# Four unused tiles that shift SBUF addresses in a fused attention and expert-layer kernel

## The chip, the cores and the metric

The kernel runs on one core of a Trainium2 chip. The metric is device time in microseconds (us) of one execution. It is given as the median of three runs. The profile is of one further execution of the same program, with its own time.

## What is computed

The reference is three layers in a row, all in fp32:

```python
# attention: B=2, H=8, S=768, D=64; key kept if pos < n_sink (4) or 0 <= rel < window (128)
scores = np.where(keep, scale * q @ k.T, -1e9)
a = softmax(scores);  x = a @ v                    # -> x: 1536 tokens x 512
# layer 1
h = (x @ w1) * (x @ w2) @ w3;  x = h @ w_out       # 512 -> 1024 -> 1024 -> 512
# layer 2
h = x @ w_in                                       # 512 -> 2048
g = np.maximum(h, 0.0) + np.log1p(np.exp(-np.abs(h)))   # softplus
return g @ w_out                                   # 2048 -> 512
```

The weights reach the chip as 64-bit floats and are decoded there.

## The kernel before

The program has an attention part and four dense stages. TensorE runs them one after the other.

- **Attention** (`attention`, to about 74 us): eight pairs of heads. Scores `s` (line 381), masking on VectorE (386), exponential on ScalarE (393), division on GpSimd (407), transposes (420) and the product with the values `xt` (456). A planner with a table of offsets sets this order.
- **Stage 1** (`stage1`): `ab` = (x w1)(x w2), 24 blocks of 24 matmuls. **Stage 2** (`stage2`): the product w34 of w3 and w_out, 8 blocks of 24. **Stage 3** (`stage3`): `x2p` = ab w34, 12 blocks of 24. **Stage 4** (`stage4`): `h` = y w_in, 48 blocks of 12, softplus on ScalarE, GpSimd and VectorE, and the output products `ox` and `o`, 48 times 12.

Every dense product is made by `mm3` (lines 164 to 168). Both operands are split into a high and a low part in the type fp32r, and three matmuls are issued per tile of 128 rows: high by high (166), high by low (167), low by high (168). There are 576 + 192 + 288 + 576 + 576 = 2,208 of these matmuls, each with 512 moving columns (2 KB a partition, read in a row) and 128 stationary columns (512 bytes a partition). So the start of either operand has the same remainder by 512 as the start of its tile; this remainder is called the rest from here on.

**Where tiles lie.** Tiles come from pools, and a pool is placed as a stack. On the left side lie `slots` (the tiles of x, later y and the output, and then those of w34) and, after the attention, `slots_ab` (ab, w_out's parts, later most of w_in and w_out of layer 2). On the right side, from the top down, lie `dec` (buffers in which weights are decoded), `ring` (five buffers `u` for decoded weights, then `bs` and `pr`) and `att` (all of the attention's tiles). After stage 3 the ring is released and `sp` (the softplus tiles spa, spu, spl, gh, gl) takes its place. All tiles of the dense stages are multiples of 2 KB, and before the change each of them starts at a rest of 480 bytes.

**Late reuse of the ring.** In stage 3 weights for stage 4 are decoded into ring buffers ahead of time (`w4_early`). When the slots come free, `w4_split` (682 to 686) copies them there: ScalarE writes the high part, VectorE the low part, both from the ring. Softplus tiles that lie on a ring buffer can't be written before that is done.

The lines of softplus are 704 (abs), 705 (exp), 706 (one plus it, on GpSimd), 709 (log), 711, 714 and 717 (VectorE), 720 (high part) and 151 (low part of anything, in VectorE).

Of the kernel before, what the change touches and what calls it, by code (L numbers as in the profile page):

```python
# [9 lines left out]
F32 = mybir.dt.float32  # L10
# [10 lines left out]
P = 128  # L21
# [38 lines left out]
    P=(-697.11, -455.77, -631.6, -474.64, -647.58, -395.71), PV=(97.88, 94.31, 94.22, 97.88, 97.88, 169.98),  # L60
# [81 lines left out]
class Net:  # L142
# [723 lines left out]
    def net(self, banded):  # L866
        tc = self.tc

        def sb(name, side="left"):
            return tc.alloc_tile_pool(name=name, bufs=1, side=side, reuse_waits="tile")  # L870

        psum = tc.alloc_tile_pool(name="psum", bufs=1, space=PSUM)
        self.slots = sb("slots")
        self.x = [[self.slot(SLOT_X + t * NC + c, f"x{t}_{c}") for c in range(NC)] for t in range(NCH)]
        self.dec = sb("dec", "right")
        self.ring = sb("ring", "right")
        att = sb("att", "right")

        if banded:
            with tc.manual_schedule():  # L880
                self.attention(att, psum)
        else:
            self.dense_attention(att, psum)
            self.last_load = ()
            self.first = self.w12_unit(0)
            self.gate = ()
        att.release()
        self.slots_ab = sb("slots_ab")
        self.w4, self.early = {}, {}
        self.stages12(self.ring, psum)  # L890
        self.stage3(psum)
        self.ring.release()
        sp = sb("sp", "right")
        self.stage4(sp, psum)
        sp.release()
        self.dec.release()
        self.slots_ab.release()
        self.slots.release()
        psum.release()
# [69 lines left out]
```

## Time and profile before

| | |
|---|---|
| median of three runs | 583.76 us (583.74 to 584.16) |
| the profiled execution | 584.81 us |
| its span, first to last instruction | 582.9 us |
| TensorE busy | 573.5 us (98%) |
| VectorE busy | 431.0 us (74%) |
| ScalarE busy | 347.1 us (60%) |
| GpSimd busy | 82.4 us (14%) |
| mean granted TensorE clock | 0.998 of the upper level |

The profile names engines PE (TensorE matmuls), PEld (TensorE weight loads), DVE (VectorE), ACT (ScalarE), POOL (GpSimd) and SP (SyncE). A duration is that of one instruction from its start to its modelled end; since matmuls are pipelined, the distance from start to start tells their rate, not the duration.

### The profile page before, as it was taken

How to read it: one execution, taken by the hardware profiler on the slowest of the kernel's cores; microseconds unless marked ns; L12 is line 12 of the kernel's file. 1: busy time of each engine (PE TensorE's matmuls, PEld its weight loads, DVE VectorE, ACT ScalarE, POOL GpSimd, SP SyncE). 2: the span in 40 equal slices, each digit the busy share in tenths (PEclk: the TensorE clock that was granted, in tenths of full speed). 3: DMA queues.
4: the chain of work that ended last, by engine and by line, in shares of the span. 5: the costliest groups of instructions: out<-in, count | busy, mean ns of one | idle time of the engine just before them, and what ended most of it. 6: DMA issues, size and time to landing. Idle time of an engine off the chain costs nothing.

```text
span 582.9 us, 9844 instructions
## 1 busy us (share of the span) xinstructions
PE 573.5 (98%) x3718; PEld 472.8 (81%) x3718; DVE 431.0 (74%) x906; ACT 347.1 (60%) x712; POOL 82.4 (14%) x162
## 2 busy tenths in 40 slices
PE   9999999999999999999999999999999999999996
PEld 6888788888888888888888777888888888888885
DVE  6889899999989976767988889845644554654553
ACT  7999967667566754545666668544444344444352
POOL 4657700000000000000000221111111011011010
PEclk9999999999999999999999999999999999999999
DMA  7566645454445523342643221000200000200002
GB/s 275 172 221 195 188 140 149 139 151 151 133 144 148 164 88 108 114 140 72 201 128 106 74 72 37 0 1 0 73 0 2 0 1 1 73 0 1 0 1 79
DMA packets 15512, 54.51 MB, mean 94 GB/s; under 512 B 1888, under 2 KB 1888, under 8 KB 15456
## 3 DMA queue, kind: packets, MB, share of 16 engines
q1 hardware_dynamic: 15168, 53.27, 29.3%
q8 instruction: 31, 0.51, 0.4%
q10 hardware_dynamic: 288, 0.52, 0.3%
q14 instruction: 25, 0.20, 0.1%
HBM read 50.64 MB, written 3.15 MB: 92 GB/s over the span
## 4 chain that ended last, share of the span: by engine, by line
PE 86%; POOL 4%; DVE 3%; ACT 3%; issue 2%; DMA 1%; SPq 0%; POOLq 0%; DVEq 0%
PE ab L166 8%; PE ab L168 7%; PE ab L167 7%; PE h L167 6%; PE h L168 6%; PE h L166 6%; PE x2p L168 4%; PE x2p L166 4%; PE x2p L167 4%; PE ox L168 3%; PE o L167 3%; PE o L168 3%; PE o L166 3%; PE ox L167 3%; PE ox L166 3%; PE w34p L168 2%
## 5 line engine op out<-in xcount | busy, mean ns | idle before, releaser
L706 POOL TENSOR_SCALAR spu<-spa 128x512 f32<-128x512 f32 (+1 forms) x49 | 35.9, 733 | 458.7 <-ACT spa L705 458.7
L151 DVE TENSOR_TENSOR gl<-spl,gh 128x512 fp32r<-128x512 f32 x47 | 32.6, 694 | 76.8 <-ACT gh L720 76.5
L704 ACT ACTIVATE spa<-h 128x512 f32<-128x512 f32 (+1 forms) x49 | 28.7, 586 | 86.5 <-PE h L168 86.3
L166 PE MATMUL ab<-x,u_w 128*128 128x512 f32 x192 | 74.8, 390 | 0.0
L167 PE MATMUL ab<-x,u_w 128*128 128x512 f32 x192 | 74.7, 389 | 0.0
L168 PE MATMUL ab<-x,u_w 128*128 128x512 f32 x192 | 74.7, 389 | 0.0
L166 PE MATMUL h<-y,w4h 128*128 128x512 f32 x192 | 74.7, 389 | 0.0
L167 PE MATMUL h<-y,w4h 128*128 128x512 f32 x192 | 74.7, 389 | 0.0
L168 PE MATMUL h<-y,w4l 128*128 128x512 f32 x192 | 74.7, 389 | 0.0
L193 ACT ACTIVATE dt_w<-raw_w 128x512 bf16<-128x512 bf16 x64 | 42.5, 669 | 52.1 <-DMA raw_w<-w4d 16.9
L201 DVE SCALAR_TENSOR_TENSOR dc_w<-raw_w,dt_w 128x512 uint16<-128x512 uint16 x64 | 44.2, 697 | 10.1 <-ACT dt_w L196 9.6
L196 ACT ACTIVATE dt_w<-dt_w,rebias 128x512 uint16<-128x512 uint16 x64 | 45.8, 721 | 1.3
L711 DVE SCALAR_TENSOR_TENSOR spu<-spu,spa 128x512 f32<-128x512 f32 (+1 forms) x49 | 33.3, 680 | 16.6 <-ACT spl L709 16.6
L709 ACT ACTIVATE spl<-spu 128x512 f32<-128x512 f32 (+1 forms) x49 | 30.4, 623 | 24.5 <-POOL spu L706 24.5
L407 POOL TENSOR_SCALAR e<-e,st 128x196 f32<-128x196 f32 (+1 forms) x96 | 39.5, 434 | 23.4 <-ACT e L393 17.1
L393 ACT ACTIVATE e<-e,st 128x196 f32<-128x196 f32 (+1 forms) x96 | 42.2, 447 | 0.9 <-DVE st L386 0.7
L168 PEld LDWEIGHTS ab<-x,u_w 128*128 128x128 f32 x192 | 36.1, 188 | 7.5
L167 PEld LDWEIGHTS h<-y,w4h 128*128 128x128 f32 x192 | 36.1, 188 | 7.5
L167 PEld LDWEIGHTS ab<-x,u_w 128*128 128x128 f32 x192 | 36.0, 188 | 7.5
L166 PEld LDWEIGHTS h<-y,w4h 128*128 128x128 f32 x192 | 36.0, 188 | 7.5
L166 PEld LDWEIGHTS ab<-x,u_w 128*128 128x128 f32 x192 | 36.0, 188 | 7.4
L168 PEld LDWEIGHTS h<-y,w4l 128*128 128x128 f32 x192 | 36.0, 188 | 7.4
(127 smaller groups left out, 1306.4 us busy)
## 6 DMA issues: line engine op xcount, KB each, us to landing
raw_w<-w4d SPq DMA_DIRECT2D x32, 511.8 KB, 4.2
raw_w<-w SPq DMA_DIRECT2D x16, 511.8 KB, 4.6
raw_w<-w3t SPq DMA_DIRECT2D x16, 511.8 KB, 3.8
qk<-qk SPq DMA_DIRECT2D x7, 792.0 KB, 4.5
raw_wo<-wod SPq DMA_DIRECT2D x8, 511.8 KB, 3.8
v<-vu SPq DMA_DIRECT2D x8, 400.0 KB, 5.5
v<-v SPq DMA_DIRECT2D x8, 384.0 KB, 4.6
out<-os SPq DMA_DIRECT2D x10, 256.0 KB, 2.3
```

The costliest lines, as they stand in the source:

```text
L151: return engine.tensor_tensor(out=lo, in0=x, in1=hi.bitcast(F32), op=ALU.subtract)
L166: nc.tensor.matmul(ps, lhs[0], rhs[0], start=start, stop=False)
L167: nc.tensor.matmul(ps, lhs[0], rhs[1], start=False, stop=False)
L168: nc.tensor.matmul(ps, lhs[1], rhs[0], start=False, stop=stop)
L193: return nc.scalar.activation(t.bitcast(BF), x["top"].bitcast(BF), AF.Abs)
L196: return nc.scalar.activation(x["t"], x["t"], AF.Relu, bias=self.rebias[:, 0:1], scale=8.0)
L201: nc.vector.scalar_tensor_tensor(out=c, in0=x["top"], scalar=0x8000, in1=t, op0=ALU.bitwise_and, op1=ALU.bitwise_or)
L393: nc.scalar.activation(e, e, AF.Exp, bias=st[:, 0, i : i + 1], scale=-1.0, accum_out=st[:, 1, i : i + 1])
L407: nc.gpsimd.tensor_scalar(out=e, in0=e, scalar1=buf("st", h)[:, 2, i : i + 1], scalar2=1.0, op0=ALU.mult, op1=ALU.mult)
L706: nc.gpsimd.tensor_scalar(out=u[:, c], in0=a[:, c], scalar1=1.0, scalar2=1.0, op0=ALU.add, op1=ALU.mult)
L709: nc.scalar.activation(l[:, c], u[:, c], AF.Ln)
L711: nc.vector.scalar_tensor_tensor(out=u[:, c], in0=u[:, c], scalar=1.0, in1=a[:, c], op0=ALU.subtract, op1=ALU.subtract)
```

## The change

Four tiles are allocated that no instruction reads or writes: 64 bytes a partition behind x in `slots`, 128 bytes at the start of `slots_ab`, 256 bytes at the end of `ring`, and 128 bytes at the end of `sp`.

```diff
         self.x = [[self.slot(SLOT_X + t * NC + c, f"x{t}_{c}") for c in range(NC)] for t in range(NCH)]
+        self.slots.tile([P, 16], F32, name="pad_w34")
         self.dec = sb("dec", "right")
...
         self.slots_ab = sb("slots_ab")
+        self.slots_ab.tile([P, 32], F32, name="pad_ab")
         self.w4, self.early = {}, {}
         self.stages12(self.ring, psum)
         self.stage3(psum)
+        self.ring.tile([P, 64], F32, name="pad_ring")
         self.ring.release()
         sp = sb("sp", "right")
         self.stage4(sp, psum)
+        sp.tile([P, 32], F32, name="pad_sp")
         sp.release()
```

The addresses of the two built programs differ like this (bytes of a partition):

| tiles | moved by | rest before | rest after |
|---|---|---|---|
| x, y, output; decode buffers | 0 | 480 | 480 |
| w34; layer 2's weights 12 to 15 | +64 | 480 | 32 |
| ab; w_out's parts; layer 2's weights 0 to 11 | +192 | 480 | 160 |
| ring buffers u, bs, pr | -256 | 480 | 224 |
| all attention tiles (qk, e, pt, v, ident, masks) | -256 | many | each by 256 other |
| softplus tiles | -128 | 480 | 352 |

Moving and stationary operand, which both had the rest 480 in every dense product, now have 480 and 224 (stage 1), 160 and 224 (stage 2), 160 and 32 (stage 3), 480 and 160 or 32 (`h`), 160 or 32 and 352 (`ox`, `o`).

On all five engines the instructions stand in the same order as before, with the same operands. One wait is new. It stands on ScalarE, at the start of stage 4, ahead of the second softplus tile (`spa0_1`; the number behind a name is only a count of tiles). Before:

```order
L157 CAST y2_3_3703<-x2p2_3_3704 128x512 [waits PE_49]
L704 ACTIVATE spa0_0_3764<-h0_0_3751 128x512 [waits DVE_49,PE_49]
L705 ACTIVATE spa0_0_3764<-spa0_0_3764 128x512 [waits Activation_49]
L709 ACTIVATE spl0_0_3766<-spu0_0_3765 128x512 [waits Pool_49]
L704 ACTIVATE spa0_1_3789<-h0_1_3776 128x512 [waits PE_49]
L705 ACTIVATE spa0_1_3789<-spa0_1_3789 128x512 [waits Activation_49]
```

And on the same engine, at the same place, now:

```order
L157 CAST y2_3_3705<-x2p2_3_3706 128x512 [waits PE_49]
L704 ACTIVATE spa0_0_3767<-h0_0_3754 128x512 [waits DVE_49,PE_49]
L705 ACTIVATE spa0_0_3767<-spa0_0_3767 128x512 [waits Activation_49]
L709 ACTIVATE spl0_0_3769<-spu0_0_3768 128x512 [waits Pool_49]
L704 ACTIVATE spa0_1_3792<-h0_1_3779 128x512 [waits DVE_49,PE_49]
L705 ACTIVATE spa0_1_3792<-spa0_1_3792 128x512 [waits Activation_49]
```

Nothing moved; line 704 on `spa0_1` now waits for VectorE too. The pools `ring` and `sp` no longer start at the same address, so this tile reaches 128 bytes into a second ring buffer, and has to wait until VectorE's `w4_split` of layer 2's weight 11 (the last of the twelve) has read it.

## Rows read from the trace of the kernel before

**Rows 1.** Span and mean granted TensorE clock of the core.

```profile
core 0: 582.9 us, clock 0.998
```

**Rows 2.** Stretches: us, busy us (instructions) of each engine, PEclk, DMA share, GB/s.

```profile
core 0: us, PE busy (x) PEld busy (x) DVE busy (x) ACT busy (x) POOL busy (x), PEclk, DMA share, GB/s
0.00:74.20 74.20, 71.22 (x1511) 58.99 (x1512) 61.89 (x292) 66.80 (x248) 46.12 (x113) 1.00 0.67 212
74.20:313.50 239.30, 239.30 (x1056) 198.22 (x1057) 207.65 (x370) 148.03 (x239) 0.31 (x1) 1.00 0.45 136
...
318.00:360.00 42.00, 40.90 (x176) 32.08 (x175) 36.57 (x61) 28.73 (x50) 10.80 (x9) 1.00 0.20 64
360.00:577.60 217.60, 217.60 (x960) 179.78 (x958) 120.73 (x181) 101.17 (x175) 24.96 (x40) 1.00 0.03 12
577.60:583.00 5.40, 0.01 (x1) 0.00 (x0) 0.69 (x1) 0.00 (x0) 0.00 (x0) 0.80 0.36 126
```

**Rows 3.** Groups of weight loads by shape: busy us, mean ns, idle before.

```profile
L166 PEld LDWEIGHTS ab<-x,u_w 128*128 128x128 f32 x192 | 36.0, 188 | 7.4
L420 PEld LDWEIGHTS pt<-ident,e 128*128 128x128 f32 x96 | 13.5, 141 | 2.1 <-POOL e L407 1.1 <-issue 0.5
L420 PEld LDWEIGHTS pt<-ident,e 128*68 128x68 f32 x80 | 9.0, 112 | 5.2 <-POOL e L407 2.8 <-issue 1.1 <-ACT pt L432 0.7
```

**Rows 4.** Single lines of the attention: duration ns, min/median/max, then first and last start.

```profile
L420 PEld LDWEIGHTS pt<-ident,e x176: 109/138/145, 10.9 to 71.1; 128*128 128x128 f32 x96, 128*68 128x68 f32 x80
L386 DVE CUSTOM_DVE_ANT_0 e<-s,bias x80: 248/356/364, 5.0 to 63.7; 128x196 f32<-128x196 f32 x64, 128x128 f32<-128x128 f32 x16
L407 POOL TENSOR_SCALAR e<-e,st x96: 370/428/939, 10.1 to 70.1; 128x196 f32<-128x196 f32 x80, 128x128 f32<-128x128 f32 x16
```

**Rows 5.** Line 151 on VectorE, several tiles: duration ns, min/median/max.

```profile
L151 DVE TENSOR_TENSOR gl<-spl,gh x47: 678/695/697, 322.5 to 569.5; 128x512 fp32r<-128x512 f32 x47
L151 DVE TENSOR_TENSOR u_w<-dr_w,u_w x30: 680/684/694, 79.0 to 216.0; 128x512 fp32r<-128x512 f32 x30
...
L151 DVE TENSOR_TENSOR y<-x2p,y x12: 681/684/693, 255.5 to 316.3; 128x512 fp32r<-128x512 f32 x12
```

**Rows 6.** VectorE in order of time, end of stage 3: start us, length us.

```profile
311.75 4.62 DVE L151 TENSOR_TENSOR w4l<-w4e,w4h 128x1024 fp32r<-128x1024 f32 x4
316.28 0.68 DVE L151 TENSOR_TENSOR y<-x2p,y 128x512 fp32r<-128x512 f32 x1
```

**Rows 7.** ScalarE in order of time, start of stage 4.

```profile
318.49 0.63 ACT L709 ACTIVATE spl<-spu 128x512 f32<-128x512 f32 x1 [0.74 <-POOL spu L706]
319.21 0.60 ACT L704 ACTIVATE spa<-h 128x512 f32<-128x512 f32 x1
```

**Rows 8.** GpSimd in order of time, start of stage 4.

```profile
323.61 0.62 POOL L706 TENSOR_SCALAR spu<-spa 128x512 f32<-128x512 f32 x1 [2.43 <-ACT spa L705]
329.53 3.12 POOL L706 TENSOR_SCALAR spu<-spa 128x512 f32<-128x512 f32 x1 [5.30 <-ACT spa L705]
...
341.96 3.05 POOL L706 TENSOR_SCALAR spu<-spa 128x512 f32<-128x512 f32 x1 [5.72 <-ACT spa L705]
...
354.31 0.64 POOL L706 TENSOR_SCALAR spu<-spa 128x512 f32<-128x512 f32 x1 [5.72 <-ACT spa L705]
```

**Rows 9.** Stretches of five us inside stage 4's start, columns as in rows 2.

```profile
345.00:350.00 5.00, 4.88 (x22) 3.69 (x20) 3.71 (x6) 3.83 (x7) 0.66 (x2) 1.00 0.31 119
350.00:355.00 5.00, 4.73 (x20) 3.62 (x21) 4.88 (x10) 4.21 (x9) 0.64 (x1) 1.00 0.00 0
355.00:360.00 5.00, 4.37 (x20) 3.29 (x19) 4.93 (x9) 3.36 (x6) 0.99 (x1) 1.00 0.34 108
```

**Rows 10.** A wait alone, on GpSimd's sequencer, line 706: ns, min/median/max.

```profile
L706 POOLq EVENT_SEMAPHORE  x47: 17/17/17, 316.4 to 565.3; - x47
```

## The prediction

> **What bounds the kernel now.** I read the granted clock first: one core, 0.998 of the upper level, so there is no disturbance to allow for [rows 1]. Then the stretches [rows 2]. From 74.2 to 313.5 us TensorE has no gap: 1,056 matmuls, which is exactly stages 1 to 3 (576 + 192 + 288), in 239.30 us. That is 226.6 ns from one start to the next. From 360 to 577.6 us there are 960 in 217.60 us, 226.7 ns each. So for 457 of 582.9 us the time is a count of matmuls times one number, and nothing that another engine does can shorten it. What is left is the attention, where TensorE stands still for 3.0 us of 74.2, the start of stage 4 (318 to 360 us, 1.1 us of standing still), and the end (5.4 us, one copy and the last store). The change counts if it changes the 226.7 ns, or lengthens something in these three places.
>
> **Part 1: the addresses of the 2,208 matmuls.** The change removes and adds no work. Its term is 2,208 times the difference in the start-to-start distance. What in the profile says whether that distance depends on rests? In the dense stages nothing can directly, because every one of the 2,208 has the same pair, 480 and 480. Three things bear on it from the side.
>
> First, other engines. In the long stretch of stages 1 to 3 VectorE is busy for 207.65 of 239.30 us (87%), ScalarE for 62% and the DMA engines for 45%; in that of stage 4 it is 55%, 46% and 3%, with 25 us of GpSimd instead of 0.3 [rows 2]. The distance is 226.6 and 226.7 ns. If accesses of others held TensorE up, less of them would show; so moving tiles against those of other engines is worth 0.
>
> Second, TensorE's own two operands, where their rests do differ. In the attention the transposes read `ident` as moving operand (rest 352), and slices of `e` as stationary one. A row of `e` is 784 bytes long and there are four buffers, so the 80 transposes of the narrow shape read from 20 different rests, and the 96 of the wide one from 24, 352 among them. If rests that agree cost anything, each shape's durations would spread. By shape the weight loads take 112 and 141 ns in the mean [rows 3], and over both shapes 109 at the least and 145 at the most [rows 4]. The spread left inside a shape is a few ns, and no place in it for a cost of some rests and not of others. This is the nearest row: same engine, same operands in fp32, other element mode and shorter.
>
> Third, the size of what could be there at all. At the upper clock level (2.4 GHz, granted 1.00 in these stretches) 226.7 ns are 544 cycles for 512 moving columns, 32 cycles or 13.3 ns more than one a column. A weight load takes 188 ns in these products [rows 3] and so has 39 ns to spare in 226.7. The bounds of this term are therefore: if all 32 cycles came from agreeing rests and went away, -2,208 x 13.3 ns = -29.4 us; if the new rests made each weight load 53 ns longer (one more cycle for each of 128 columns, 188 to 241 ns), it would no longer hide, and each matmul would come 14.6 ns later, +32.2 us. I take 0, by the transposes, to which it is nearest.
>
> A rule of the Trainium skill speaks against that value: the page "TensorE: Matmul & The Clock Gate", section "Wait — 56ns, not 53.3ns?", gives N / 2.4 GHz + about 2.5 ns, 215.7 ns for 512 columns back to back. The trace doesn't agree with it (226.7). If its number were what these matmuls do without a collision, the sum would be an estimated 2,208 x 11.0 = 24.3 us lower, at 559.5. The same page, in "Step-by-step: what each phase is for", gives TensorE two separate SBUF read ports, one for each operand, by which the excess is no collision and the sum stays; the transposes agree with this.
>
> **Part 2: VectorE, ScalarE and GpSimd.** Within the attention all tiles move by the same 256 bytes, and within softplus all by 128; so the rests inside an instruction keep their distance there, and only those of the dense stages change, such as `u` (224) against the decode buffers (480). The rows say that this costs nothing either way: line 151 with two SBUF inputs at one rest takes 684 ns (`u_w`) and, with one input from PSUM, 684 ns (`y`) [rows 5]. The mask step writes `e` at 20 rests, with a median of 356 and at most 364 ns; GpSimd's division, at 24 rests, has a median of 428 ns [rows 4] (the minima are those of the narrower shape). These engines also have room: what ends last in these stages is TensorE. The term is 0, and the cover is TensorE's row without gaps. Without that cover the worst spread, 684 to 695 ns in line 151 [rows 5], would cost 11 ns in each of some 900 VectorE instructions, 10 us that fall on an engine that is idle for 32 and 97 us in the two stretches.
>
> **Part 3: the new wait.** ScalarE's line 704 on `spa0_1` now waits for VectorE's fourth `w4_split`. In the trace the four end at 311.75 + 4.62 = 316.37 us [rows 6], and line 704 starts at 319.21 [rows 7]. The wait is fulfilled 2.84 us before it is asked. What stays is one more instruction on ScalarE's sequencer, 17 ns by the row of GpSimd's [rows 10], at a place where ScalarE has just ended line 709 (318.49 + 0.63 = 319.12). Behind it on ScalarE's queue are lines 704, 705, 709 and 720 of this tile, and GpSimd's 706 waits for them. TensorE waits 1.1 us in all for that chain, so between 0 and 0.02 us; I take 0.
>
> **Part 4: who comes first, GpSimd or VectorE.** Between 318 and 360 us line 706 takes 0.62 us, but 3.12 and 3.05 us where it starts in a burst of VectorE's decoding, and 0.64 us in a third burst at 354.31 [rows 8]. Which of them happens hangs on tenths of a us. The change brings a few ns into this. One long 706 fewer gives back at most TensorE's whole standing still there, 1.10 us [rows 2]; one more costs up to 3.12 - 0.64 = 2.5 us. I take 0, since no duration ahead of it changes.
>
> **The sum.** Against the profiled execution (584.81 us, of which 582.9 are span and 1.9 lie around it): 0 + 0 + 0 + 0, so 584.8 for a profiled execution. This one was 1.05 us above the median of the runs shown, 583.76; against the median the forecast is 583.8 us.
>
> **The rivals.**
>
> *Rests count for fp32r matmuls (faster).* Place: all dense stages, at once. For it: an excess of 32 cycles a matmul, and no dense matmul in the trace with other rests. Against it: the transposes; and that the excess is the same 32 cycles in both stretches, with other tiles and with more or less work beside it [rows 2]. Time: 583.8 - 29.4 = 554.4 if all goes, 583.8 - 576 x 13.3 ns = 576.1 if only the distance of 256 in stage 1 does it. 3 in 100.
>
> *A long 706 more (slower).* Place: GpSimd's line 706 at 354.31, in the third burst, which was short by chance. TensorE has no reserve left there: it stands still for 0.12, 0.27 and 0.63 us in the stretches from 345, 350 and 355 us [rows 9]. So from the point at which GpSimd's start falls behind VectorE's by some 0.1 us, nearly all of 2.5 us is added: 586.3. For it: the other two bursts. Against it: nothing that runs ahead of it is changed by more than 0.02 us. 4 in 100.
>
> *The new rests collide where the old ones didn't (slower).* It decides from a weight load of 188 + 39 ns on. 14.6 ns on the 2,208 give 616.0, on the 576 of `h` alone 592.2. 2 in 100.
>
> *The change doesn't do what it says.* In part it doesn't: the distance of rests inside the attention and inside softplus stays. Its result is that of the forecast, 583.8, and is counted there.
>
> Small effects without a name get 2 in 100 on the faster and 1 on the slower side.
>
> **How the numbers follow.** "The same" means within 0.2% (1.17 us), about what a measurement of this kernel can tell from no change. The forecast has 88 in 100, faster 3 + 2 = 5, slower 4 + 2 + 1 = 7. The range needs none of the large rivals to hold 8 in 10: it covers -1.1 us of part 4 and half of its other side, with the scatter of the runs (583.74 to 584.16): 582.7 to 585.0 us.
>
> **What would show it.** The two stretches without gaps: 1,056 and 960 matmuls at 226.6 to 226.7 ns again. Any other number there decides part 1 at once, stage by stage, since each has its own pair of rests. Line 151 at 684 ns on `u_w`; no idle time of ScalarE for VectorE at line 704; TensorE standing still for about 3.0, 1.1 and 5.4 us; two long 706. I am wrong if the distance moves by more than 0.5 ns (1.1 us over 2,208), or if a third 706 is long or one of the two is short and TensorE's 1.1 us follows it.

## The result: 1.1% slower; in three of the four dense stages a matmul comes 3 to 7 ns later

The changed kernel takes 590.81 us in the median of 4 runs (590.5 to 591.23); the kernel before took 583.96 us beside it (583.74 to 585.04, 4 runs). The ratio is 1.0109, with a 95% interval of 1.0088 to 1.013. The forecast was 583.8 us, no change, in a range that ended at 585.0. It was wrong.

The span of the profiled execution grew from 582.9 us [rows 1] to 588.6, at full granted clock:

```profile
core 0: 588.6 us, clock 1.000
```

The two stretches without gaps were to decide part 1 [rows 2]. After, they hold fewer matmuls in the same time, with TensorE as busy as before. The third row is the start of stage 4, where TensorE now stands still for 0.04 us instead of 1.10. (Columns as in [rows 2].)

```profile
core 0: us, PE busy (x) PEld busy (x) DVE busy (x) ACT busy (x) POOL busy (x), PEclk, DMA share, GB/s
74.20:313.50 239.30, 239.28 (x1046) 195.36 (x1043) 206.68 (x370) 146.75 (x239) 1.30 (x1) 1.00 0.44 135
360.00:577.60 217.60, 217.60 (x944) 176.99 (x943) 119.60 (x179) 100.76 (x173) 25.19 (x41) 1.00 0.03 10
318.00:360.00 42.00, 41.96 (x183) 33.89 (x182) 37.84 (x61) 29.96 (x52) 5.18 (x8) 1.00 0.20 63
```

From 360 us there are 944 where 960 stood: 217.60 us / 944 = 230.5 ns from start to start, not 226.7. No new gap, no new wait: the distance itself became longer. A reader who looks only at the busy share (100% in both kernels) sees nothing.

**By stage.** A window from the first matmul of a block to the first of the next gives the distance of that block alone. First the kernel before: the first part of stage 2 (72 matmuls), a stage-1 part (72), the rest of stage 2 (120), the rest of stage 1 (216), and stage 3 (288). The weight loads' count is that of the block's matmuls, give or take one; the matmuls' count has one or two that began earlier.

```profile
core 0: us, PE busy (x) PEld busy (x) DVE busy (x) ACT busy (x) POOL busy (x), PEclk, DMA share, GB/s
139.49:155.81 16.32, 16.32 (x74) 13.52 (x72) 15.75 (x29) 11.06 (x20) 0.00 (x0) 1.00 0.55 170
155.81:172.13 16.32, 16.32 (x74) 13.52 (x72) 14.65 (x28) 10.18 (x18) 0.00 (x0) 1.00 0.49 153
172.13:199.33 27.20, 27.20 (x122) 22.53 (x120) 24.89 (x44) 17.95 (x31) 0.00 (x0) 1.00 0.46 130
199.33:248.29 48.96, 48.96 (x218) 40.55 (x216) 37.15 (x67) 26.70 (x44) 0.00 (x0) 1.00 0.36 114
248.29:313.57 65.28, 65.28 (x290) 54.07 (x288) 53.39 (x87) 38.14 (x54) 0.00 (x0) 1.00 0.47 142
```

The same five blocks after:

```profile
139.73:156.53 16.80, 16.80 (x74) 13.48 (x73) 16.30 (x30) 11.23 (x19) 0.00 (x0) 1.00 0.50 157
156.53:173.18 16.65, 16.63 (x73) 13.44 (x72) 14.88 (x29) 10.75 (x19) 0.00 (x0) 1.00 0.53 158
173.18:201.18 28.00, 28.00 (x121) 22.45 (x120) 25.39 (x46) 17.76 (x31) 0.00 (x0) 1.00 0.42 123
201.18:250.35 49.17, 49.17 (x217) 40.48 (x216) 37.43 (x67) 27.08 (x44) 0.00 (x0) 1.00 0.37 115
250.35:317.28 66.93, 66.93 (x289) 54.31 (x288) 54.91 (x88) 38.02 (x54) 0.00 (x0) 1.00 0.45 140
```

Each block of before has 226.67 ns (16.32 / 72, 27.20 / 120, 48.96 / 216, 65.28 / 288). After, stage 2 has 233.3 (16.80 / 72, 28.00 / 120) and stage 3 has 232.4 (66.93 / 288), while stage 1 in its last part has 227.6 (49.17 / 216, the first few matmuls of it longer), nearly as before. Stage 1 is the one whose two rests differ by 256. In stage 4, by single starts and without the waits, `h` has about 231 ns and the output products about 230.

**Where the 5.7 us of span come from.** The end of stage 3 moved from 313.57 to 317.28, 3.71 us: 0.22 in the attention (its end went from 74.08 to 74.30), 0.56 in stage 1, 1.28 in stage 2 and 1.65 in stage 3. The start of the last matmul moved from 577.22 to 583.18, 5.96 us, so stage 4 added 2.25 only. Its 1,152 matmuls at 230.5 instead of 226.7 ns make 4.4 us; the 2.1 us missing from this are mostly waits that before's profiled execution had and this one hasn't, the 1.06 us of the third row above among them. GpSimd at the start of stage 4 shows them: the two ops of line 706 that took 3.12 and 3.05 us [rows 8] take 0.71 each. Counted from the end of stage 3, the first starts at the same place within 0.1 us, the second 1.2 us earlier:

```profile
333.30 0.71 POOL L706 TENSOR_SCALAR spu<-spa 128x512 f32<-128x512 f32 x1 [5.30 <-ACT spa L705]
344.46 0.71 POOL L706 TENSOR_SCALAR spu<-spa 128x512 f32<-128x512 f32 x1 [5.31 <-ACT spa L705]
```

Whether the change took the long ops away isn't shown. In the experiments e3, e4 and e6 below, which lose nothing, e3 and e4 have no long op here either, and e6 has one, at the first of the two places:

```profile
329.82 3.11 POOL L706 TENSOR_SCALAR spu<-spa 128x512 f32<-128x512 f32 x1 [5.31 <-ACT spa L705]
```

Each kernel has one profiled execution only. e3, without a long op, has a span of 581.4 us. Against that the span grew by 7.2 us, which is close to the 6.85 us between the medians, and to 2,208 matmuls x 3.4 ns (226.7 to 230.1 in the mean of all stages, without waits) = 7.5 us.

**The duration of a matmul grows, that of its load doesn't.** By shape (busy us, mean ns of one, idle before), after:

```profile
L166 PE MATMUL h<-y,w4h 128*128 128x512 f32 x192 | 75.7, 394 | 0.0
L166 PE MATMUL ab<-x,u_w 128*128 128x512 f32 x192 | 75.0, 391 | 0.0
L166 PE MATMUL x2p<-ab,w 128*128 128x512 f32 x96 | 37.9, 395 | 0.0
L166 PEld LDWEIGHTS h<-y,w4h 128*128 128x128 f32 x192 | 36.1, 188 | 8.1
```

And before, the same matmuls:

```profile
L166 PE MATMUL h<-y,w4h 128*128 128x512 f32 x192 | 74.7, 389 | 0.0
L166 PE MATMUL ab<-x,u_w 128*128 128x512 f32 x192 | 74.8, 390 | 0.0
L166 PE MATMUL x2p<-ab,w 128*128 128x512 f32 x96 | 37.3, 389 | 0.0
```

The load stays at 188 ns [rows 3]. The matmul's duration, whose end is modelled, is 5 to 6 ns longer in `h` and `x2p`, and 1 ns in stage 1.

**What stayed, as forecast.** Line 151 on VectorE has the medians of [rows 5] within 2 ns, although the rest of `u` against the decode buffers changed. (The tiles of `y` didn't move, and those of `gl`, `spl` and `gh` moved together.) The rows after:

```profile
L151 DVE TENSOR_TENSOR gl<-spl,gh x47: 677/696/697, 326.3 to 575.1; 128x512 fp32r<-128x512 f32 x47
L151 DVE TENSOR_TENSOR u_w<-dr_w,u_w x30: 679/686/695, 80.5 to 218.5; 128x512 fp32r<-128x512 f32 x30
L151 DVE TENSOR_TENSOR y<-x2p,y x12: 683/685/692, 257.5 to 319.0; 128x512 fp32r<-128x512 f32 x12
```

The new wait of ScalarE is fulfilled long before. The last `w4_split` on VectorE ends at 317.85 + 1.23 = 319.08 us; line 704 on `spa0_1` starts at 322.99, directly behind line 709:

```profile
317.85 1.23 DVE L151 TENSOR_TENSOR w4l<-w4e,w4h 128x1024 fp32r<-128x1024 f32 x1 [0.16 <-ACT w4h L685]
322.25 0.63 ACT L709 ACTIVATE spl<-spu 128x512 f32<-128x512 f32 x1 [0.74 <-POOL spu L706]
322.99 0.60 ACT L704 ACTIVATE spa<-h 128x512 f32<-128x512 f32 x1
```

### The profile page after: what moved, and what is told of

It reads as the page before. It is cut to its first block, busy times and chain, and to the rows that moved or that the text cites. A ratio compares the mean times of both kernels' runs of the same rounds, so it can differ in the third digit from the quotient of the medians.

```text
span 588.6 us, 9845 instructions
## 1 busy us (share of the span) xinstructions
PE 580.4 (99%) x3718; PEld 473.5 (80%) x3718; DVE 432.0 (73%) x906; ACT 347.9 (59%) x712; POOL 76.8 (13%) x162
## 4 chain that ended last, share of the span: by engine, by line
PE 93%; ACT 3%; POOL 3%; DVE 1%; issue 0%; POOLq 0%; DVEq 0%
PE ab L166 7%; PE ab L168 7%; PE ab L167 7%; PE h L168 7%; PE h L166 7%; PE h L167 7%; PE ox L166 4%; PE x2p L168 4%; PE x2p L167 4%; PE ox L168 4%; PE x2p L166 4%; PE o L166 4%; PE ox L167 4%; PE o L167 4%; PE o L168 4%; PE w34p L168 3%
## 5 line engine op out<-in xcount | busy, mean ns | idle before, releaser
L706 POOL TENSOR_SCALAR spu<-spa 128x512 f32<-128x512 f32 (+1 forms) x49 | 30.4, 620 | 468.3 <-ACT spa L705 468.3
```

Of the source, the lines that this page charges most:

```text
L706: nc.gpsimd.tensor_scalar(out=u[:, c], in0=a[:, c], scalar1=1.0, scalar2=1.0, op0=ALU.add, op1=ALU.mult)
```

## The experiments

The theory, formed from the table by stage: the distance of a matmul hangs on its own two operands, on the **difference** of the address of the moving minus that of the stationary one, and 256 bytes count as none. Its rivals: that the rest of one operand alone decides; that other engines get in the way at the new addresses; that the unused tiles do something else (the new wait, the order); that the period is 128 or 512 and not 256.

Each kernel differs from before or after by unused tiles or a few lines, so the same blocks can be read off. A time without a number of runs is that of one execution. Differences are written modulo 256 below: after has 0 in stage 1, 192 in stage 2, 128 in stage 3, 64 or 192 in `h` and in the outputs.

**e1: one tile of the four.** Only w34, ab, w_out's parts and layer 2's weights move, by 64: difference 64 in stage 2 and the outputs, 192 in `h`, 0 in stages 1 and 3.

```diff
         self.x = [[self.slot(SLOT_X + t * NC + c, f"x{t}_{c}") for c in range(NC)] for t in range(NCH)]
+        self.slots.tile([P, 16], F32, name="pad_w34")
```

> Only the unused tile behind x, of 64 bytes: w34, ab, w_out's parts and layer 2's weights move by 64, nothing else; no order and no wait changes. Pair theory (the start-to-start distance of the dense matmuls hangs on the difference of the rests, moving minus stationary operand, with period 256; read from the changed kernel: 226.7 ns at 0, about 229.7 at 64, 232.4 at 128, 233.3 at 192): stages 1 and 3 have difference 0 and stay at 226.7 ns; stage 2 and the output products have +64, 229.7 ns; h has -64, that is 192, 233.4 ns. Sum 192 x 3.0 + 576 x 6.7 + 576 x 3.0 ns = 6.2 us, 590.1 us. Single theory (an operand's own rest counts, 480 is good and 32 is not): stage 3, with both operands moved to 32, gets slower too, by some ns. Other-engines theory (rests against what VectorE, ScalarE and DMA touch count): stage 1 changes too, since ab is written at another rest there, and h and outputs change alike.

Measured: 590.89 us, against 583.86 of before on the same chip. The first row is the rest of stage 2 (120), the second stage 3 (288).

```profile
173.09:200.58 27.49, 27.49 (x122) 22.46 (x120) 24.13 (x43) 17.28 (x30) 0.00 (x0) 1.00 0.42 124
250.16:315.49 65.33, 65.33 (x290) 54.07 (x289) 53.52 (x87) 38.03 (x54) 0.00 (x0) 1.00 0.46 142
```

229.1 ns (27.49 / 120) in stage 2 and 226.8 in stage 3, where both operands moved together by 64; stage 1 226.9 and `h` 233.4 by single starts, without the waits. So one unused tile of 64 bytes costs as much as all four, and only in those stages whose operands it moves apart.

**e2: the same by 32 bytes** (`[P, 8]`).

> The same with 32 bytes. Pair theory: stages 1 and 3 at 226.7 ns; stage 2 and outputs (+32) between 226.7 and 229.7 ns; h (-32, that is 224) between 226.7 and 233.4 ns; total 584 to 590 us. A distance under 226.7 ns anywhere would mean that equal rests are not the best ones. Single theory: stage 3 changes as well.

Measured: 592.05 us. Rest of stage 2, then stage 3:

```profile
172.67:200.67 28.00, 28.00 (x121) 22.49 (x120) 26.10 (x47) 17.54 (x30) 0.00 (x0) 1.00 0.48 145
249.68:314.98 65.30, 65.30 (x289) 54.05 (x288) 54.59 (x88) 37.98 (x54) 0.00 (x0) 1.00 0.45 143
```

Stage 2 has 233.3 ns at a difference of 32, more than at 64; a smaller difference doesn't cost less. This size was missed by the expectation, and with it the total of 584 to 590 us. Stage 3, at 0, has 226.7.

**e3: all dense tiles moved, differences 0.** Everything that the stages read has the rest 32 instead of 480.

```diff
+        self.dec.tile([P, 112], F32, name="pad_dec")
...
+            const.tile([P, 16], F32, name="pad_const")
```

> Everything moves by the same rest: 64 bytes more ahead of the left side's pools, 448 bytes more below the decode buffers on the right, so every operand of the dense products lies at rest 32 instead of 480, and all differences stay 0. Pair theory: all stages 226.7 ns, 583.9 us, no change. Single theory: all stages get slower by 3 to 7 ns a matmul, 2,208 of them, 590 to 599 us.

Measured: 584.04 us in the median of 10 (583.3 to 585.92), ratio 1.0006 (0.9993 to 1.002). Rest of stage 2, stage 3, a stretch of stage 4:

```profile
172.43:199.63 27.20, 27.20 (x122) 22.53 (x120) 24.64 (x44) 17.59 (x31) 0.00 (x0) 1.00 0.43 129
248.69:313.98 65.29, 65.29 (x290) 54.08 (x289) 54.02 (x88) 38.02 (x54) 0.00 (x0) 1.00 0.46 143
360.00:570.00 210.00, 210.00 (x928) 173.95 (x927) 116.16 (x173) 97.61 (x169) 24.60 (x40) 1.00 0.03 11
```

All as before. Moving both operands' rests from 480 to 32 costs nothing, so it is the pair that matters.

**e4: the ring and softplus tiles by 256.** Difference 256 in stages 1 and 2 and in the outputs; the tiles of w34 and ab stay.

```diff
+        self.ring.tile([P, 64], F32, name="pad_ring")
         self.ring.release()
...
+        sp.tile([P, 64], F32, name="pad_sp")
         sp.release()
```

> Unused tiles of 256 bytes at the end of ring and of the softplus pool alone: ring buffers and softplus tiles move by -256, so stages 1 and 2 and the output products have a difference of 256, stage 3 and h 0. The attention moves by -256 as in the changed kernel. Pair theory with period 256: all stages 226.7 to 226.9 ns, 583.9 us. With period 512: stage 2 and the outputs slower by some ns (768 x 3 to 7 ns, 586 to 589 us), stage 1 as in the changed kernel. If the attention's move costs anything it shows here alone: the changed kernel's attention ends as in before, so 0.

Measured: 583.98 us (583.33 to 585.23, 10 runs), ratio 1.0005 (0.9995 to 1.0015), with 226.7 to 226.8 ns in every stage, waits left out. A difference of 256 is as good as none.

**e5: after without softplus.** If other engines got in TensorE's way, work taken from them would shorten the distance. Here `gh` and `gl` are made of `h` itself, so VectorE and ScalarE lose about three quarters of their work in stage 4 and GpSimd all of it.

```diff
-        for c in cuts:
-            nc.scalar.activation(a[:, c], ps[:, c], AF.Abs)
...
-            self.last_hi = nc.scalar.copy(gh[:, c], l[:, c])
-            self.lo_dve(gl[:, c], l[:, c], gh[:, c])
+            self.last_hi = nc.scalar.copy(gh[:, c], ps[:, c])
+            self.lo_dve(gl[:, c], ps[:, c], gh[:, c])
```

> The changed kernel with the softplus left out (stage 4 splits h itself into a high and a low part; exponential, log, GpSimd's step and three VectorE steps are gone, so the output is not the network's). All four unused tiles and all addresses stay as in the changed kernel. Pair theory (TensorE's two operands alone decide, nothing of other engines): in the stretch of stage 4 the start-to-start distance stays at 230 to 231 ns in the mean, though VectorE, ScalarE and GpSimd do a third of the work or none. Other-engines theory: it goes back to 226.7 ns, or most of the way, in stage 4 alone.

Measured: 590.26 us. Stage 4:

```profile
360.00:577.60 217.60, 217.60 (x944) 176.84 (x943) 31.28 (x47) 25.65 (x45) 0.00 (x0) 1.00 0.03 10
```

VectorE has 31.28 us instead of 119.60, ScalarE 25.65 instead of 100.76, GpSimd nothing; the matmuls are 944 in the same time, as in after. The theory of other engines falls, for stage 4.

**e6: the change itself, with 256 bytes in all four tiles.** Four unused tiles at the same places, but all differences are 0 or 256.

```diff
+        self.slots.tile([P, 64], F32, name="pad_w34")
...
+        self.slots_ab.tile([P, 64], F32, name="pad_ab")
...
+        self.ring.tile([P, 64], F32, name="pad_ring")
...
+        sp.tile([P, 64], F32, name="pad_sp")
```

> The four unused tiles stay, but each is made 256 bytes long: x lies at rest 480, w34 at 224, ab at 480, ring and softplus at 224, so the differences of moving and stationary operand are 0 or 256 everywhere. Pair theory with period 256: 226.7 ns in all stages, 583.9 us, the whole loss of the changed kernel (6.9 us) gone with the four tiles still there. If unused tiles as such cost something, or a difference of 512 is needed: 586 to 591 us.

Measured: 584.79 us (583.12 to 585.84, 10 runs) against 584.47 of before, ratio 1.0006 (0.9992 to 1.002). Rest of stage 2, and the stretch of stage 4:

```profile
172.41:199.61 27.20, 27.20 (x121) 22.53 (x120) 25.19 (x45) 17.75 (x31) 0.00 (x0) 1.00 0.45 135
360.00:570.00 210.00, 210.00 (x927) 173.71 (x926) 116.54 (x173) 98.44 (x170) 24.97 (x40) 1.00 0.03 11
```

The whole loss is gone. It was the sizes of the unused tiles, not that they are there.

**e7 and e8: the tile of e1 with 96 and with 128 bytes** (`[P, 24]`, `[P, 32]`).

> The tile behind x alone, of 96 bytes: stage 2 and outputs at +96, h at -96 (160 by a period of 256), stages 1 and 3 at 0. Pair theory: stages 1 and 3 at 226.7 ns; the others between 229 and 234 ns as at 32, 64, 128 and 192; total 588 to 592 us. A value under 226.7 ns at +96 or +160 would be a placement better than equal rests.

> The tile behind x alone, of 128 bytes: stage 2, outputs and h all at 128 by a period of 256, stages 1 and 3 at 0. Pair theory: 232.4 ns in stage 2, h and outputs, as stage 3 of the changed kernel had with the difference 128; total 583.9 + 1,344 x 5.7 ns = 591.6 us. If the period were 128: 226.7 ns everywhere, 583.9 us.

Measured: 592.74 us and 592.47 us, against 584.47. The rest of stage 2 in e7 and in e8, one row of each:

```profile
172.71:200.73 28.02, 28.02 (x122) 22.53 (x120) 26.01 (x46) 17.39 (x30) 0.00 (x0) 1.00 0.49 145
```

```profile
173.30:201.29 27.99, 27.99 (x121) 22.52 (x120) 26.20 (x48) 17.78 (x31) 0.00 (x0) 1.00 0.49 149
```

233.5 and 233.3 ns; `h` 233.6 and 233.1 by single starts. Both totals lie a little above what was expected. A period of 128 is excluded by e8; one of 512 was excluded by e4 and e6. Only 64 is milder (229 to 230 ns, in e1 as in stage 4 of after).

**e9: the same products in fp32.** The forecast had taken its value from transposes in fp32. Here stage 2 (difference 128) and stage 3 (difference 0) issue their matmuls with both operands read as fp32, on e8's addresses.

```diff
+        lhs, rhs = [x.bitcast(F32) for x in lhs], [x.bitcast(F32) for x in rhs]
...
-            self.mm3(ps, (u[:, 0, k], u[:, 1, k]), wo, kt == 0, kt == NF - 1)
+            self.mm3w(ps, (u[:, 0, k], u[:, 1, k]), wo, kt == 0, kt == NF - 1)
```

> The tile behind x alone, of 128 bytes, as in the run before with it, and the matmuls of stages 2 (difference 128) and 3 (difference 0) read the same operands as fp32 instead of fp32r, as the attention's matmuls do; the other stages stay. The time is longer by far, since fp32 takes two passes; what counts is the distance in stage 2 against that in stage 3. If the cost of rests is one of fp32r alone (its moving operand streams one column a cycle, fp32 one in two by the attention's 109 ns for 128 columns): about 430 ns a matmul in both, equal within 1 ns, which would be why the attention showed nothing. If it holds for any type: stage 2 longer by 6 to 13 ns a matmul than stage 3.

Measured: 893.32 us. Each matmul now has two records, two passes. The first row is stage 2's first part (144 passes), the second stage 3 (576):

```profile
140.26:202.06 61.80, 61.80 (x146) 27.36 (x145) 26.10 (x45) 17.26 (x28) 0.00 (x0) 1.00 0.22 73
370.37:617.57 247.20, 247.20 (x578) 109.44 (x576) 56.08 (x88) 39.82 (x54) 0.00 (x0) 1.00 0.12 38
```

61.80 / 144 = 429.2 ns at 128, 247.20 / 576 = 429.2 ns at 0, per pass and not per matmul as expected. In fp32 a difference of 128 costs nothing.

**e10: 64 instead of 128 stationary columns** in 23 of 24 matmuls of each block of stages 2 and 3, on e8's addresses. If the two streams collide only while both run, a load that is half as long should cost half.

```diff
...
+        c = slice(0, 64)
+        nc.tensor.matmul(ps[c], lhs[0][:, c], rhs[1], start=False, stop=False, skip_group_check=True)
+        nc.tensor.matmul(ps[c], lhs[1][:, c], rhs[0], start=False, stop=stop, skip_group_check=True)
```

> The tile behind x alone, of 128 bytes, and in stages 2 (difference 128) and 3 (difference 0) 23 of 24 matmuls of a block load 64 stationary columns instead of 128, so half of their product is left out. If the 32 cycles above 512 are made by the weight load's reads beside the stream (32 lines of 16 bytes in 512 bytes would be one reading of that number): stage 3 at 512 + 16 cycles, 220.0 ns, and stage 2's excess over 213.3 ns halved as well, from 19.9 to about 10 ns, 223 ns. If they are a fixed cost of each matmul: 226.7 ns in stage 3, and stage 2 keeps 6 ns more than it, 232 to 234 ns.

Measured: 591.36 us. Rest of stage 2 (difference 128), stage 3 (difference 0):

```profile
172.69:200.24 27.55, 27.55 (x122) 16.41 (x120) 25.05 (x45) 18.07 (x31) 0.00 (x0) 1.00 0.44 131
249.25:315.46 66.21, 66.21 (x290) 39.28 (x288) 54.48 (x88) 38.02 (x54) 0.00 (x0) 1.00 0.46 141
```

229.6 and 229.9 ns: better at 128, but **worse at 0**, where 226.7 stood. Both readings that I had set against each other missed. A shorter load doesn't simply collide less.

**e11: a few bytes, either way.** The stationary slices of the kernel before start 4 bytes off in stage 1, 8 in stage 2, 16 in stage 3, 24 in `h`, 48 in the outputs. If some small difference gave less than 226.7 ns, a faster kernel could be built of it.

```diff
+    def off(self, i, c):
+        c = c if i < 3 else -c
+        return slice(i * P + c, (i + 1) * P + c)
...
-                    k = slice(ct * P, (ct + 1) * P)
+                    k = self.off(ct, 1)
```

> All tiles lie as in the kernel before (every rest 480), but each slice of 128 stationary columns is taken some columns further on for three of four slices, and as many back for the fourth: 1 column (4 bytes) in stage 1, 2 (8 bytes) in stage 2, 4 (16 bytes) in stage 3, 6 (24 bytes) in h, 12 (48 bytes) in the outputs. So the products use the wrong weights, and only the distances count. No order and no wait changes. If the cost comes by lines of 16 or 32 bytes that both operands read: stage 1 and 2 keep 226.7 ns, or nearly, and the rest rise to 229 to 234 ns, as 32 bytes did (233.4). If any inequality breaks the regular spacing: all stages at 228 to 234 ns. If equal rests are not the best placement, one of the stages falls below 226.7 ns.

Measured: 594.95 us against 585.66. Stage 1's first part (288 matmuls), rest of stage 2, stage 3:

```profile
74.56:141.69 67.13, 67.13 (x291) 54.12 (x289) 63.12 (x121) 45.51 (x80) 0.98 (x1) 1.00 0.47 137
175.15:202.99 27.84, 27.84 (x122) 22.56 (x120) 25.49 (x46) 17.31 (x30) 0.00 (x0) 1.00 0.47 139
253.27:320.11 66.84, 66.84 (x290) 54.32 (x288) 54.46 (x88) 38.26 (x54) 0.00 (x0) 1.00 0.47 140
```

233.1, 232.0 and 232.1 ns. Four bytes are enough, and no difference tried is below 226.7. So nothing in these runs beats the kernel before.

All together, in ns from start to start:

| difference modulo 256 | ns | from |
|---|---|---|
| 0 (0 or 256 bytes) | 226.7 to 226.9 | before, e3, e4, e6; stages 1 and 3 of e1, e2, e7, e8 |
| 4, 8, 16, 24, 48 either way | 231 to 233.1 | e11 |
| 32 and 224 | 233.3, 233.6 | e2, stage 2 and `h` |
| 64 | 229 to 230 | e1, stage 2 and outputs; after, `h` and outputs with the first twelve weights |
| 96, 128, 160, 192 | 232.0 to 233.6 | e7 and e8; `h` and outputs of e9 and e10; e1's `h`; after, stages 2 and 3, `h` and outputs with the last four weights |

These are means over whole blocks, waits left out, and they hide a pattern. At some differences the single distances repeat in a fixed order: 231, 231, 238 ns in the rest of stage 2 of e7, 238 and 229 ns by turns in that of e8. Nor does the difference alone fix the mean. `h` has the same addresses in e8, e9 and e10, but 233.1 ns in e8 and 232.0 in e9 and e10. The same stretch of stage 4 in e8 and then in e10, where 907 matmuls fit instead of 903:

```profile
360.00:570.00 210.00, 210.00 (x903) 169.10 (x902) 113.73 (x168) 94.68 (x160) 23.50 (x38) 1.00 0.03 11
360.00:570.00 210.00, 210.00 (x907) 170.36 (x906) 113.54 (x168) 94.78 (x161) 23.23 (x38) 1.00 0.03 11
```

So with all 128 columns loaded, the difference decides whether the 226.7 ns are reached; what is paid beyond them depends on something more, which no run here isolates.

## Why the prediction was wrong

**The step that failed** is the last sentence of part 1, "I take 0, by the transposes, to which it is nearest". The transposes are fp32 with other shapes. e9 shows that in fp32 even the dense matmuls don't feel a difference of 128. Taking them for the nearest row, as the same engine with operands in fp32, passed over the data type of the dense products, fp32r. In the same matmuls at the same addresses the type changes the answer (e8 and e9); whether by itself, or because a pass of 429.2 ns leaves the load more room, is open. The step also read durations of weight loads. Those stay at 188 ns in after too, so in fp32r they would have shown nothing either. A row that could not show the effect was read as proof that there is none. What the runs show in place of the 0 is 3.4 ns a matmul in the mean, 7.5 us by the traces, 6.85 between the medians. The bounds of that term, -29.4 and +32.2 us, did hold these +7.5 us; the range had been cut to what the proxy allowed.

**A row that did speak was overlooked.** The argument took 226.7 ns as one number, because the averages of both stretches agreed. Single starts in the kernel before show that it is a pace that TensorE reaches only some matmuls after a wait. Behind the wait that ends at 357.36 us:

```profile
357.36 0.50 PE L168 MATMUL ox<-w4h,gl 128*128 128x512 f32 x1 [0.63 <-DVE gl L151]
357.69 0.39 PE L166 MATMUL ox<-w4h,gh 128*128 128x512 f32 x1
357.92 0.39 PE L167 MATMUL ox<-w4l,gh 128*128 128x512 f32 x1
358.15 0.40 PE L168 MATMUL ox<-w4h,gl 128*128 128x512 f32 x1
358.39 0.39 PE L166 MATMUL o<-w4h,gh 128*128 128x512 f32 x1
```

The distances in ns from there on, worked out from the unrounded starts, and below them those in after from 172.95 us, the last matmul of a stage-1 part and then stage 2:

```
before: 337 230 231 236 228 233 231 226 227 227 226 227 227 226 227 227
after:  228 233 233 234 233 233 233 234 234 233 232 235 233 232 234 233
```

Before needs seven matmuls here to reach 226/227/227, in the mean exactly 544 cycles at 2.4 GHz, and stays there. Behind other long waits of before, e3, e4 and e6 it needs three to ten. After, at a difference of 192, doesn't reach it in all of stage 2. So the same matmul already took 228 to 236 ns in the trace of before, with the same addresses: the pace wasn't fixed by the instruction's size alone; what else set it, that trace doesn't say. That was reason enough not to give "the same" 88 in 100.

**The rivals.** *The new rests collide where the old ones didn't* had the sign and laid the cost on the pair of rests, at 2 in 100. Its place was right in part: stage 1, at a difference of 256, pays nothing. Its mechanism and price were off: it waited for the load to grow beyond 227 ns and gave 14.6 ns a matmul. The load stays at 188 ns and the matmuls come 3 to 7 ns later. *Rests count for fp32r matmuls (faster)* had the right operands and the wrong sign: the equal rests of before are the best of all that was tried, and the 32 cycles over one per column are there at every difference.

**What the other steps said.** "First, other engines": worth 0, and e5 shows it for stage 4. Part 2, VectorE and ScalarE: 0, as line 151 on `u_w` shows. Part 3, the new wait: 0. Part 4, line 706: the change made none longer. But the forecast's own sign came true: both long ops are short in after, and TensorE's 1.10 us of standing still went to 0.04. Among the kernels without a loss there are two long ops in before, one in e6 and none in e3 and e4, so they come and go without this change too, and the times of e3, e4 and e6 stand at 1.0005 to 1.0006 of before's. The attention grew by 0.22 us, which is scatter: with its tiles where before has them, it ends at 74.81 us in e1 and at 74.75 in e8.

**The two reads and the 2.5 ns.** In fp32, with the difference at 128 and at 0, the pass is the same 429.2 ns (e9); in fp32r, with nothing but 64 bytes between the operands' tiles, the matmul comes 2.4 to 6.7 ns later (e1, stage 2 and `h`). By "TensorE: Matmul & The Clock Gate", section "Step-by-step: what each phase is for", in the Trainium skill, loading the next weights takes no SBUF read bandwidth from the running matmul. For fp32 the runs agree with it (e9). For fp32r a cost that hangs on where the one operand lies against the other doesn't fit it, and the measurement decides. The 2.5 ns a matmul on top of one column a cycle, which the same page of the Trainium skill gives in "Wait — 56ns, not 53.3ns?", doesn't fit fp32r (226.7 ns against 215.7) at any address tried. Two cycles a column make 426.7 ns for a pass in fp32, an estimate from 512 columns at 2.4 GHz. With the 2.5 ns of that section of the Trainium skill the estimate is 429.2, and that is what e9 measured.

**What stays open.** That the load of the weights and the moving stream meet somewhere, with a period of 256 bytes, is what the runs suggest, since the difference counts and not one rest; which load it is (the running tile's or the next one's) and what they share was not shown. e10 speaks against the simple form of it. Why 64 is milder than 32 and 128, and 192 isn't, is open too. bf16 wasn't tried.

## What to carry to other kernels

In a kernel whose time is a count of fp32r matmuls like these (512 moving and 128 stationary columns), lay the tiles so that moving and stationary operand start at the same remainder by 256 bytes: a small tile of 32 or 64 bytes put between pools cost 1.2 to 1.4% here, though no instruction touches it, and padding by 256 cost nothing that ten runs could tell. Before calling a start-to-start distance a constant, read single starts behind a wait, not the mean over a stage: a pace that settles can also be lost. And a row of another data type, or of another quantity (the load's duration instead of the distance of the starts), says little about the cost of a pair of addresses.

## What the hardware showed that I had not expected

- The distance of a 512-column fp32r matmul hangs on the difference of its operands' addresses modulo 256 bytes: 226.7 ns at 0, 229 to 233.6 in the mean elsewhere, and 4 bytes suffice (e11, 233.1).
- With difference 0 it settles three to ten matmuls after a long wait; the mean is then exactly 544 cycles. At some other differences it settles too, into a repeating order with a higher mean (231, 231, 238 ns in e7).
- The weight load's duration (188 ns) shows nothing of it; the matmul's modelled duration does (389 to 395 ns).
- In fp32 each matmul is two passes of 429.2 ns, at any difference tried (0 and 128).
- With 64 stationary columns the regular pace is lost at difference 0 as well (229.9 ns, e10).
